# The opening of a gated linear attention and SiLU kernel in another order: pair 1's decays ahead of pair 0's logarithm

## The chip, the cores and the metric

The kernel runs on one core of a Trainium2 chip. The metric is the device time of one execution in microseconds (us); the times given are medians over several runs. TensorE (PE) does matrix products and transposes, VectorE (DVE) and ScalarE (ACT) read the accumulators in PSUM, GpSimd (POOL) works on SBUF alone, and SyncE (SP) issues most of the loads and stores. ACT and POOL issue a few as well.

## The reference

```python
def _attn_ref(q, k, v, f_logit):            # (4, 8, 768, 48) each
    f = 1.0 / (1.0 + np.exp(-f_logit))
    for t in range(S):
        state = f[:, :, t, :, None] * state + np.einsum('bhd,bhe->bhde', k[:, :, t], v[:, :, t])
        y[:, :, t] = np.einsum('bhd,bhde->bhe', q[:, :, t], state)

def _moe_ref(x, w_in, w_out):               # x (3072, 384), w_in (384, 2048), w_out (2048, 384)
    h = x @ w_in
    g = h * (1.0 / (1.0 + np.exp(-h)))
    return g @ w_out
```

x is y with the heads side by side. So each of 4 batches and 8 heads carries a 48x48 state that decays by a gate f per channel and takes up k v at each step, and the result goes through a two-layer network with SiLU.

## The kernel before

The sequence of 768 steps is cut into chunks of 128 steps (six per batch, 24 in all), and the chunks are worked on in twelve **pairs** (`PAIRS`). Pairs 0 to 3 are of kind T: the two chunks are the first two of one batch, loaded together with two neighbouring steps in one partition. The others are of kind N: the same chunk of two batches. A chunk is named by its pair and 0 or 1, so `a.1.0` is of pair 1, first chunk.

Within a chunk the recurrence becomes matrix work. The steps, with their names in the plan:

- `f`, `k`, `q`, `v`: loads (L228). `E` and `L`: exp(-f) and log(1 + that) on ACT (L234, L238), for a whole pair at once. `cs`: the running sum of the logs as a product with a triangular matrix (L305, and small products L309 that give the chunk's whole decay).
- `a`, `ia`, `al`: exponentials of that sum on ACT (L317, L256), the decays. `qg` = q times a, `ki` = k times ia (L322), written to `qk`.
- `tq`: transposes on TensorE (L329); `qkc`: the copy of them out of PSUM (L333). `sc`: the scores (L346); `at`: scores times the causal mask (L354). `vb`: v in bf16 (L184 or L182).
- `y`: the masked scores times v (L263); `yi`: the part that comes from the state before (L362). `d`: what the chunk adds to the state (L275); `sd` and `su`: the new state (L389, L387, L393).
- `yc`, `yT`, `xc`: copy, transpose and copy that give xT. `mi`: xT times w_in (L249), eight pieces of six matmuls for each pair. `si`: SiLU (L254). `mo`: times w_out (L286), `oc` and `so`: copy and store.
- `wi`, `wo`: the four requests each that bring w_in and w_out, issued by POOL (L207, L210); they turn f32 into bf16 on the way. `wi.n` feeds `mi.P.2n` and `mi.P.2n+1`.
- `idle.512.n`: n matmuls on zeros, with 512 columns each (L436).

The order of all this is the text `PLAN`, written out word by word and emitted as it stands (`manual_schedule`). A word is name, engine and buffer slot: `k.1.0:S:4` loads k of pair 1 from SP into slot 4 of k; A is ACT, V is DVE, G is POOL, P is TensorE. Each engine does its own words in the order of the plan; waits between engines, and waits for a slot whose last reader isn't done, follow from the data. An idle word names the PSUM bank that it writes. Each class of buffers has a number of slots (`SLOTS`: four for f, six for k, q and v, eight PSUM banks `pb`).

Two lines in the emission matter here. The first four loads of the plan are issued ahead of everything else, the others at their place; and the table of exp and log is loaded on ACT between the two (L457):

```python
        loads = [t for t in plan if t[0] in SRC][:4]
        for t in loads:
            run(*t)
        nc.scalar.preload_act_table_set(TABLES["exp"])
```

The load of f of pair 1 is in two halves, `f.1.0` from SP and `f.1.1` from ACT, and `E.1.0` needs both. A switch of ACT's table between exp and SiLU is put ahead of the first word that needs the other one (L485).

Of the kernel before, what the change touches and what calls it, by code (L numbers as in the profile page):

```python
# [55 lines left out]
oc.0.0:A:1 q.3.0:S:1 mo.1.0.3:P: oc.1.0:A:2 oc.1.1:V:3 qg.3.0:V:1 mi.2.6:P:4 al.5.1:A:2 qg.5.0:V:2 k.5.1:S:1 a.5.1:A:1 mi.2.0:P:1 mi.2.1:P:7
mi.2.2:P:3 q.5.1:S: qg.5.1:V:3 ia.5.1:A:2 al.5.0:A:3 a.3.1:A:4 qg.3.1:V: k.5.0:S: ia.5.0:A:0 ki.5.1:G: v.3.0:S:0 ia.3.0:A:1 ki.3.0:V: mi.2.5:P:5
tq.3.1:P:2 qkc.3.1:V:1 si.2.1:A:0 ki.5.0:G: si.2.2:A: si.2.0:A: su.2.1:G:0 mi.2.3:P:6 tq.3.0:P:0 si.2.3:A: mi.2.4:P:2 qkc.3.0:V: mi.2.7:P:1
mo.2.1.0:P:6 mo.2.1.1:P: vb.3.1:G:0 si.2.4:A: vb.3.0:V:1 d.3:P:2,0 sd.3.0:V:0 su.3.0:G:0 si.2.5:A: v.5.0:S:1 si.2.6:A: sc.3.1:P:4,5 sc.3.0:P:3,7
at.3.0.0:V:0 si.2.7:A: mo.2.1.2:P: mo.2.1.3:P: vb.5.0:G:2 at.3.1.0:V:1 mo.2.0.0:P:3 mo.2.0.1:P: mo.2.0.2:P: f.4.0:S:1 E.4.0:A:0 sd.3.1:V:0 f.6.0:S:0  # L60
qkD.5.1:S:0 at.3.1.1:V: qkD.5.0:S:1 oc.2.1:A:4 L.4.0:A:0 cs.4.1:P:5 E.6.0:A:1 L.6.0:A:1 at.3.0.1:V: v.5.1:S: sc.5.0:P:7,6 y.3:P:0,4 sc.5.1:P:2,1
at.5.0.0:V:2 yi.3.1:P: a.4.1:A:0 yc.3.0:A:0 at.5.1.1:V:0 mo.2.0.3:P: at.5.0.1:V: yc.3.1:A:1 oc.2.0:A:5 al.4.1:A:1 d.5.0:P:0 cs.6.0:P:4 a.6.0:A:1
al.6.0:A:4 yT.3.0:P:1 cs.4.0:P:7 xc.3.0:V:0 ia.6.0:A:2 yT.3.1:P:3 xc.3.1:V: q.4.0:S:1 cs.6.1:P:6 q.4.1:S: su.3.1:G:0 at.5.1.0:V: y.5.0:P:1 ia.4.1:A:4
a.6.1:A:3 mi.3.7:P:3 vb.5.1:G:0 k.4.1:S:1 ki.4.1:V:2 d.5.1:P:2 y.5.1:P:5 al.6.1:A:0 yc.5.0:A:1 yT.5.0:P:1 xc.5.0:A:1 sd.5.0:V:0 su.5.0:G:0 v.4.1:S:0
vb.4.1:G:0 mi.3.6:P:4 al.4.0:A:5 yc.5.1:V:0 yT.5.1:P:5 xc.5.1:V: ia.6.1:A:4 mi.3.3:P:1 si.3.3:A:0 q.6.0:S:0 mi.3.1:P:5 si.3.7:A: mi.5.5:P:6 si.3.6:A:
mi.3.0:P:0 mi.5.4:P:3 k.6.0:S:0 ki.6.0:G:3 mi.3.2:P:4 sd.5.1:V:1 si.5.5:A:1 mi.5.6:P:6 qg.4.1:V: si.3.0:A: mi.5.2:P:0 mi.5.7:P:1 si.5.4:A: mi.3.5:P:3
si.3.2:A: si.3.1:A: mo.3.1.0:P:5 a.4.0:A:0 mi.5.3:P:4 mo.3.1.1:P: mi.3.4:P:2 ia.4.0:A:2 si.5.2:A: v.6.0:S:2 k.4.0:S: vb.6.0:V:2 si.3.5:A: ki.6.1:G:0
mi.5.0:P:7 mi.5.1:P:3 su.5.1:G:0 mo.3.0.0:P:0 vb.6.1:V:1 si.5.6:A: d.4.1:P:6 qg.6.0:G: si.3.4:A: ki.4.0:G:1 mo.3.1.2:P: qg.4.0:V: d.6.1:P:2 v.4.0:S:
si.5.7:A: si.5.3:A: so.0.1:S: vb.4.0:A:3 si.5.1:A: d.4.0:P:4 mo.3.0.1:P: mo.3.0.2:P: sd.4.0:V:1 sd.4.1:V:0 mo.3.0.3:P: qg.6.1:G: si.5.0:A:
mo.5.0.0:P:6 mo.5.0.1:P: f.9.0:S:0 so.1.1:S: mo.3.1.3:P: f.7.0:S:1 oc.3.1:V:3 E.7.0:A:1 qkD.4.1:S:0 L.7.0:A:1 cs.7.1:P:4 mo.5.0.2:P: qkD.4.0:S:1  # L70
oc.3.0:V:0 q.7.0:S:0 sc.4.0:P:5,7 at.4.0.1:V:0 k.7.0:S:1 at.4.0.0:V: sc.4.1:P:3,1 at.4.1.0:V:2 E.9.0:A:0 al.7.1:A:2 mo.5.1.0:P:0 mo.5.1.1:P:
mo.5.1.2:P: at.4.1.1:V: y.4.0:P:3 L.9.0:A:0 ia.7.1:A:3 ki.7.1:V:1 a.7.1:A:0 cs.9.0:P:5 al.9.0:A:3 a.9.0:A:2 y.4.1:P:1 su.4.0:G:0 yc.4.1:V:0
mo.5.1.3:P: d.6.0:P:7 yc.4.0:A:1 so.2.1:S: qg.7.1:G: yT.4.0:P:1 qkD.6.0:S:2 xc.4.0:V:1 sd.6.0:V:1 su.4.1:G:0 oc.5.1:A:4 cs.7.0:P:3 al.7.0:A:5
a.7.0:A:3 cs.9.1:P:4 al.9.1:A:1 qg.7.0:G:3 ia.7.0:A:0 yT.4.1:P:0 mo.5.0.3:P: xc.4.1:V: mi.4.4:P:0 mi.4.7:P:7 a.9.1:A:1 mi.4.2:P:1 ia.9.0:A:4 so.3.0:S:
sd.6.1:V:0 oc.5.0:V:0 qkD.6.1:S:3 ia.9.1:A:3 sc.6.0:P:6,2 at.6.0.0:V:2 at.6.0.1:V: sc.6.1:P:5,3 mi.4.5:P:4 mi.4.6:P:6 si.4.5:A:1 mi.4.0:P:2 si.4.4:A:
v.7.0:S:0 vb.7.0:G:0 si.4.2:A: at.6.1.1:V:0 mi.4.1:P:3 at.6.1.0:V: y.6.1:P:1 ki.7.0:V: yc.6.1:V:0 mi.4.3:P:5 y.6.0:P:0 yc.6.0:V:1 yT.6.1:P:1 d.7.0:P:4
su.6.1:G:0 xc.6.1:V:1 su.6.0:G:0 vb.7.1:G:2 si.4.0:A: v.8.0:S:2 vb.8.1:G:1 si.4.7:A: sd.7.0:V:0 si.4.1:A: q.9.0:S:1 mo.4.1.0:P:3 si.4.3:A:
mo.4.0.0:P:0 mo.4.0.1:P: mo.4.1.1:P: mo.4.1.2:P: mo.4.0.2:P: qg.9.1:V:0 si.4.6:A: mo.4.0.3:P: f.8.0:S:0 E.8.0:A:0 L.8.0:A:0 cs.8.1:P:4 so.3.1:S:
ia.8.1:A:1 d.7.1:P:1 sd.7.1:V:1 cs.8.0:P:6 ia.8.0:A:0 mo.4.1.3:P: qkD.7.0:S:0 oc.4.0:A:3 yD.6.0:S: mi.6.2:P:1 al.8.0:A:4 qg.9.0:G:2 sc.7.0:P:0,5
# [438 lines left out]
```

## Time and profile before

| | before |
|---|---|
| time, median of 3 runs | 177.46 us (177.25 to 177.75) |
| span of the profiled execution, first to last instruction | 175.6 us |
| median of the runs less that span | 1.9 us |
| TensorE busy | 169.4 us, 96% of the span |
| ACT busy | 129.8 us, 74% |
| DVE busy | 81.2 us, 46% |
| POOL busy | 61.2 us, 35% |
| read from HBM, written | 25.17 MB, 4.72 MB |

The profile shows one execution. Its page gives the busy time of each engine; sums over stretches give the same for a part of the span, with the mean share of the 16 DMA engines; the chain of waits follows the work that ended last back from the last instruction; the order of time lists instructions by engine, merged where neighbours are alike (x6 is six in a row), with the idle time ahead of them and what ended it in brackets. Busy time of TensorE holds the idle matmuls too. A DMA's row on SPq, ACTq or POOL is its issue, not its transfer; landing times are in rows of their own. The profile gives no time of its own beside the span, so the 1.9 us are the difference to the median.

### The profile page before, as it was taken

What the parts mean: (1) busy time and instruction counts of PE and PEld (TensorE: products, weight loads), DVE (VectorE), ACT (ScalarE), POOL (GpSimd) and SP (SyncE); (2) the same over time, 40 slices, a digit from 0 to 9 for tenths busy, and PEclk for the clock granted to TensorE, in tenths of its full rate; (3) what the DMA queues carried; (4) which work ended last, traced back from release to release, by engine and by line L of the source; (5) the groups of instructions that cost most, each with busy time, mean ns of one, the idle gap of its engine ahead of it and who ended that gap; (6) DMA issues with size and microseconds to landing.
All of it is one profiled execution on the core that took longest, in us unless ns stands there. A gap on an engine that the chain in (4) does not pass through costs nothing.

```text
span 175.6 us, 4754 instructions
## 1 busy us (share of the span) xinstructions
PE 169.4 (96%) x1927; PEld 125.2 (71%) x1930; DVE 81.2 (46%) x166; ACT 129.8 (74%) x239; POOL 61.2 (35%) x104
## 2 busy tenths in 40 slices
...
GB/s 146 320 325 265 211 216 201 188 182 240 232 172 164 210 208 158 228 183 217 128 230 166 143 236 158 205 188 231 225 128 183 193 191 230 54 61 118 90 4 90
DMA packets 110677, 32.12 MB, mean 183 GB/s; under 512 B 104096, under 2 KB 110528, under 8 KB 110656
## 3 DMA queue, kind: packets, MB, share of 16 engines
...
q8 instruction: 15, 0.25, 0.6%
q14 instruction: 6, 0.05, 0.1%
HBM read 25.17 MB, written 4.72 MB: 170 GB/s over the span
## 4 chain that ended last, share of the span: by engine, by line
PE 79%; ACT 11%; DVE 5%; DMA 2%; issue 2%
PE pb L286 35%; PE pb L249 29%; ACT x L317 3%; ACT hT L254 3%; PE pb L350 3%; ACT L485 2%; DVE qk L322 2%; DMA f<-in_f_logit_dram 2%; PE pb L362 2%; PE pb L366 2%; PE pb L346 1%; PE pb L312 1%; PE pb L383 1%; PE pb L374 1%; DVE atm L354 1%
## 5 line engine op out<-in xcount | busy, mean ns | idle before, releaser
L249 PE MATMUL pb<-xT,w_in_sb 128*128 128x256 bf16 x576 | 69.1, 272 | 0.3 <-ACT hT L254 0.2
L286 PE MATMUL pb<-w_out_sb,hT 128*128 128x384 bf16 (+2 forms) x400 | 68.6, 320 | 0.0
L249 PEld LDWEIGHTS <-w_in_sb 128*128 128x128 bf16 x576 | 54.8, 98 | 9.0 <-issue 0.8
L254 ACT ACTIVATE hT<-pb 128x512 bf16<-128x512 f32 x96 | 50.5, 611 | 10.9 <-PE pb L249 10.7
L286 PEld LDWEIGHTS <-hT 128*128 128x128 bf16 x400 | 37.2, 98 | 20.5 <-issue 0.2
L393 POOL TENSOR_TENSOR st<-sd,al 48x192 bf16<-48x192 f32 x40 | 21.4, 535 | 59.0 <-PE pb L362 33.4
L354 DVE TENSOR_TENSOR atm<-pb,triu 128x512 bf16<-128x512 f32 x32 | 20.1, 684 | 11.2 <-PE pb L350 6.6
L317 ACT ACTIVATE x<-pb 128x384 f32<-128x384 f32 x48 | 21.0, 501 | 5.4 <-PE pb L305 3.0
L485 ACT ACT_TABLE_LOAD x17 | 21.8, 1283 | 0.3
L184 DVE COPY ob<-pb 128x384 f32<-128x384 f32 (+1 forms) x11 | 5.7, 528 | 27.3 <-PE pb L286 27.3
L387 DVE TENSOR_TENSOR sd<-pb,st 128x384 f32<-128x384 f32 x16 | 8.8, 552 | 11.8 <-PE pb L383 10.3
L322 POOL TENSOR_TENSOR qk<-q,x 128x384 bf16<-128x384 f32 x11 | 10.9, 996 | 9.0 <-ACT x L317 6.1
L322 POOL TENSOR_TENSOR qk<-k,x 128x384 bf16<-128x384 f32 x11 | 11.8, 1081 | 5.7 <-ACT x L317 2.4
L182 ACT COPY ob<-pb 128x384 f32<-128x384 f32 (+1 forms) x14 | 6.7, 477 | 8.5 <-PE pb L286 8.1
L234 ACT ACTIVATE e<-f 128x768 f32<-128x768 f32 x12 | 10.1, 840 | 3.8 <-DMA f<-in_f_logit_dram 3.7
L322 DVE TENSOR_TENSOR qk<-q,x 128x384 bf16<-128x384 f32 x13 | 8.2, 648 | 7.2 <-ACT x L317 7.1
L354 DVE TENSOR_TENSOR atm<-pb,mask 128x512 bf16<-128x512 f32 x16 | 10.1, 684 | 1.6 <-issue 1.0
L436 PE MATMUL pb<-zero,triu 128*128 128x512 bf16 (+1 forms) x26 | 9.0, 449 | 1.4 <-POOL triu masks.py:66 1.4
L184 DVE CAST yb<-pb 128x384 bf16<-128x384 f32 x14 | 7.6, 554 | 5.1 <-PE pb L366 2.6
L184 DVE COPY qkTT<-pb 128x1024 bf16<-128x1024 bf16 x7 | 4.6, 683 | 11.0 <-PE pb L329 11.0
L322 DVE TENSOR_TENSOR qk<-k,x 128x384 bf16<-128x384 f32 x13 | 9.0, 707 | 1.0 <-DMA k<-in_k_dram 0.8
L184 POOL CAST vb<-v 128x384 bf16<-128x384 f32 x12 | 6.4, 535 | 8.0 <-DMA v<-in_v_dram 7.7
...
## 6 DMA issues: line engine op xcount, KB each, us to landing
f<-in_f_logit_dram SPq DMA_DIRECT2D x11, 384.0 KB, 5.1
k<-in_k_dram SPq DMA_DIRECT2D x10, 384.0 KB, 5.5
q<-in_q_dram SPq DMA_DIRECT2D x10, 384.0 KB, 5.4
v<-in_v_dram SPq DMA_DIRECT2D x10, 384.0 KB, 4.9
...
w_in_sb<-in_moe_w_in_dram POOLq DMA_DIRECT2D x4, 384.0 KB, 8.6
w_out_sb<-in_moe_w_out_dram POOLq DMA_DIRECT2D x4, 384.0 KB, 10.5
...
```

The lines of the kernel that those rows point to most:

```text
L184: ENG[eng].tensor_copy(dst, src)
L234: return nc.scalar.activation(e, at("f", P)[:, j * w:(j + 1) * w], AF.Exp, scale=-1.0)
L249: nc.tensor.matmul(h[:, i, cols], w_in_sb[:, kk, n * 128:(n + 1) * 128], at("xT", P)[:, kk, cols], start=(kk == 0), stop=(kk == KT - 1))
L254: return nc.scalar.activation(at("hT", P)[:, 2 * j:2 * j + 2, :], at("h", P, j).rearrange("p (n c) -> p n c", n=2), AF.Silu)
L286: nc.tensor.matmul(at("o" + key, P, i)[:, 0:cols.stop - cols.start], at("hT", P)[:, n, i * C:(i + 1) * C], w_out_sb[:, n, cols], start=(n ...
L317: nc.scalar.activation(at(kind, P, i).rearrange("p h d -> p (h d)"), at("cs", P, i)[:, 0:HD], AF.Exp, scale=1.0 if kind == "ia" else -1.0)
L322: ENG[eng].tensor_mul(at("qk", P, i)[:, j, :, 0:D], heads("qk"[j], P, i), at("ia" if j else "a", P, i))
L354: ENG[eng].tensor_mul(at("atm", P, i)[:, r], at(f"s{r}", P, i).rearrange("p (n c) -> p n c", c=C), mask[:, None, :].to_broadcast([C, NP, C]))
L387: nc.vector.tensor_add(at("sd", P, i), d_ps, prev_state(P, i))
L393: nc.gpsimd.tensor_mul(at("st", P, i)[lo:lo + D, :, r * D:(r + 1) * D], at("sd", P, i)[lo:lo + D, :, r * D:(r + 1) * D], al_of(P, i)[lo:lo ...
L436: nc.tensor.matmul(buf["pb", int(got)][:, 0:rest[0]], triu, zero[:, 0:rest[0]], start=True, stop=True, skip_group_check=True)
L485: nc.scalar.preload_act_table_set(turns[n])
```

## The change

Only `PLAN` changes, and in it only the opening, some 235 words of 846; the 610 words from `v.3.0` on are the same in the same order, in other line breaks. The core of the diff:

```diff
-f.1.0:S:0 f.1.1:A: E.1.0:A:0 L.1.0:A:0 idle.512.10::0 cs.1.1:P:0 f.0.0:S:1 E.0.0:A:1 k.1.0:S:0 L.0.0:A:1 idle.512.1::1 cs.1.0:P:1
-q.1.0:S:0 idle.512.2::2 cs.0.0:P:2 idle.256.1::3 cs.0.1:P:3 a.1.1:A:0 qg.1.1:V:0 a.1.0:A:1 ia.1.1:A:2 ki.1.1:V: idle.512.1::4 tq.1.1:P:4 ia.1.0:A:3
-ki.1.0:V:1 v.1.0:S:0 f.2.0:S:0 qg.1.0:V: idle.512.3::5 tq.1.0:P:1 vb.1.1:V:0 vb.1.0:G:1 d.1:P:5,6 qkc.1.1:V:0 qkc.1.0:V: idle.512.1::7 idle.256.1::7
-sc.1.0:P:1,4 ia.0.0:A:0 k.0.0:S:1 ki.0.0:V:0 at.1.0.0:V:0 at.1.0.1:V: idle.512.2::7 idle.256.1::7 sc.1.1:P:7,1 at.1.1.0:V:1 at.1.1.1:V: a.0.1:A:2
-ia.0.1:A:3 sd.1.0:A:0 wi.1:G: al.1:A:0 E.2.0:A:1 L.2.0:A:1 q.0.0:S:1 a.0.0:A:1 qg.0.0:V: idle.512.1::5 cs.2.0:P:0 cs.2.1:P:5 al.2:A:1 ia.2.1:A:0
-su.1.0:G:0 ia.2.0:A:4 al.0:A:2 a.2.0:A:1 qg.0.1:V:1 idle.512.2::2 y.1:P:1,7 tq.0.0:P:4 v.0.0:S:1 yc.1.0:V:0 a.2.1:A:2 qkc.0.0:A:1 sd.1.1:V:0 wi.3:G:
-ki.0.1:G: tq.0.1:P:3 qkc.0.1:V: yT.1.0:P:1 yi.1.1:P: yc.1.1:A:0 wi.0:G: idle.512.2::2 sc.0.1:P:3,4 vb.0.1:G:0 at.0.1.0:V:0 yT.1.1:P:7 xc.1.0:A:0
-sc.0.0:P:6,5 at.0.0.1:V:1 at.0.0.0:V: vb.0.0:A:1 wi.2:G: idle.512.1::2 d.0:P:3,1 xc.1.1:A: sd.0.0:A:1 su.0.0:G:0 mi.1.2:P:7 mi.1.3:P:3 at.0.1.1:V:
-y.0:P:4,6 q.2.0:S:0 yc.0.0:A:0 yi.0.1:P: wo.0:G: mi.1.6:P:5 yT.0.0:P:4 sd.0.1:V:1 su.0.1:G:0 xc.0.0:A:1 wo.1:G: yc.0.1:V:1 yT.0.1:P:6 xc.0.1:V:
-qg.2.1:G:0 mi.1.7:P:1 k.2.0:S:0 si.1.7:A:0 mi.0.3:P:6 mi.0.7:P:4 wo.2:G: si.1.6:A: mi.0.6:P:0 mi.0.1:P:1 si.0.1:A:1 wo.3:G: su.1.1:G:0 si.0.6:A:
-mi.0.0:P:5 mi.0.2:P:2 si.0.2:A: mi.1.0:P:1 ki.2.1:V: si.1.3:A: mi.1.4:P:0 si.1.4:A: si.0.0:A: si.1.2:A: mi.0.5:P:2 mi.1.5:P:3 si.0.5:A: mi.0.4:P:0
-mi.1.1:P:7 mo.0.1.0:P:2 v.2.0:S:0 si.1.5:A: mo.0.0.0:P:3 si.1.0:A: si.1.1:A: mo.1.0.0:P:7 mo.1.1.0:P:1 mo.1.0.1:P: mo.1.1.1:P: qg.2.0:V:1 f.3.0:S:0
-si.0.3:A: mo.0.1.1:P: si.0.7:A: ki.2.0:V: tq.2.0:P:4 qkc.2.0:V:1 tq.2.1:P:6 mo.0.0.1:P: si.0.4:A: qkc.2.1:V: mo.1.1.2:P: sc.2.1:P:6,4 sc.2.0:P:0,5
-at.2.0.0:V:0 at.2.0.1:V: mo.1.0.2:P: mo.0.0.2:P: at.2.1.0:V:1 at.2.1.1:V: mo.0.1.2:P: mo.0.1.3:P: vb.2.0:G:0 vb.2.1:A:1 d.2:P:6,5 sd.2.0:V:0 E.3.0:A:1
...
+f.1.0:S:0 k.1.0:S:4 idle.512.10::4 q.1.0:S:1 f.0.0:S:1 f.1.1:A: E.1.0:A:0 L.1.0:A:0 idle.512.1::0 idle.256.1::0 cs.1.0:P:6 a.1.0:A:2 cs.1.1:P:0
+al.1:A:1 v.1.0:S:1 qg.1.0:V:0 ia.1.0:A:4 vb.1.0:G:2 ia.1.1:A:0 ki.1.0:V: ki.1.1:V:2 a.1.1:A:1 qg.1.1:V: E.0.0:A:0 idle.512.5::1 idle.256.1::1
+tq.1.0:P:6 qkc.1.0:V:1 idle.512.1::1 tq.1.1:P:5 L.0.0:A:0 idle.256.1::1 cs.0.0:P:2 ia.0.0:A:4 wi.1:G: vb.1.1:G:0 k.0.0:S:1 wi.3:G: qkc.1.1:V:
+sc.1.0:P:0,7 at.1.0.1:V:2 sc.1.1:P:4,5 at.1.1.0:V:0 cs.0.1:P:1 f.2.0:S:0 at.1.1.1:V: q.0.0:S:1 ki.0.0:G:4 a.0.0:A:2 ia.0.1:A:3 E.2.0:A:1 a.0.1:A:0
+v.0.0:S:4 d.1:P:2,7 at.1.0.0:V: idle.512.5::3 y.1:P:4,3 qg.0.0:G: qg.0.1:V:2 wi.0:G: L.2.0:A:1 tq.0.0:P:6 q.2.0:S:4 k.2.0:S:3 cs.2.0:P:5 ki.0.1:V:
+sd.1.0:A:0 tq.0.1:P:2 al.0:A:0 su.1.0:G:0 cs.2.1:P:1 yc.1.0:A:2 yT.1.0:P:0 qkc.0.0:V:0 qkc.0.1:V: ia.2.0:A:1 xc.1.0:V:3 yi.1.1:P: a.2.0:A:4 wi.2:G:
+vb.0.0:V:1 sc.0.1:P:2,4 v.2.0:S:5 a.2.1:A:0 yc.1.1:A:0 vb.0.1:G:3 al.2:A:4 idle.256.1::6 yT.1.1:P:6 ia.2.1:A:2 sc.0.0:P:5,1 d.0:P:3,0 at.0.1.1:V:1
+at.0.1.0:V: xc.1.1:A: mi.1.2:P:4 at.0.0.1:V:2 mi.1.3:P:6 at.0.0.0:V: y.0:P:5,1 yc.0.0:V:2 sd.0.0:A:0 su.0.0:G:0 yi.0.1:P: wo.0:G: wo.1:G: mi.1.6:P:2
+si.1.3:A:0 f.3.0:S:3 sd.1.1:V:1 yc.0.1:A:1 yT.0.0:P:5 yT.0.1:P:6 xc.0.1:V:1 mi.1.7:P:3 xc.0.0:A: si.1.7:A: si.1.2:A: sd.0.1:V:0 f.5.0:S:2 si.1.6:A:
+mi.0.3:P:5 mi.0.0:P:0 mi.0.2:P:7 mi.0.7:P:4 mi.0.1:P:6 mi.1.4:P:1 mi.1.5:P:3 si.1.4:A: si.0.1:A:1 ki.2.0:V:1 mi.0.5:P:2 si.0.0:A: mi.1.0:P:6 si.0.5:A:
+mi.0.4:P:0 mi.1.1:P:1 si.1.5:A: si.0.2:A: si.1.0:A: si.1.1:A: mo.0.1.0:P:2 mo.0.0.0:P:3 wo.2:G: mo.1.0.0:P:7 mi.0.6:P:6 si.0.6:A: mo.1.1.0:P:1
+si.0.3:A: si.0.7:A: ki.2.1:G:4 mo.1.0.1:P: qg.2.1:V: qg.2.0:V: mo.1.1.1:P: mo.0.1.1:P: tq.2.0:P:4 qkc.2.0:V:1 tq.2.1:P:6 mo.0.0.1:P: wo.3:G: si.0.4:A:
+qkc.2.1:V: mo.1.1.2:P: sc.2.1:P:6,4 sc.2.0:P:0,5 at.2.0.0:V:0 at.2.0.1:V: mo.1.0.2:P: mo.0.0.2:P: at.2.1.0:V:1 at.2.1.1:V: mo.0.1.2:P: mo.0.1.3:P:
+vb.2.0:G:0 vb.2.1:A:1 d.2:P:6,5 su.0.1:G:0 sd.2.0:V:0 y.2:P:4,0 mo.1.1.3:P: oc.0.1:V:0 mo.0.0.3:P: E.3.0:A:1 L.3.0:A:1 cs.3.0:P:2 yc.2.0:V:1 E.5.0:A:0
+L.5.0:A:0 a.3.0:A:4 su.2.0:G:0 sd.2.1:V:0 q.5.0:S:0 yi.2.1:P: yc.2.1:A:0 yT.2.0:P:4 cs.3.1:P:6 al.3:A:0 ia.3.1:A:1 cs.5.0:P:5 xc.2.0:V:0 a.5.0:A:0
...
```

What differs, engine by engine:

- **SP**: the first four loads are f.1.0, k.1.0, q.1.0 and f.0.0 (before: f.1.0, f.1.1, f.0.0, k.1.0). f.1.1 is no longer one of them, so ACT issues it after L457. k.0.0 goes ahead of f.2.0. Slots are other ones: q.0.0 takes slot 1, which was q.1.0's; k.1.0, v.0.0, q.2.0, k.2.0, v.2.0 and f.3.0, f.5.0 take slots that nothing has used (before, q.2.0, k.2.0, v.2.0, f.3.0 and f.5.0 took used ones).
- **ACT**: a.1.0, al.1, ia.1.0, ia.1.1 and a.1.1 stand ahead of E.0.0 and L.0.0 (before: behind). sd.1.0 moves from ahead of E.2.0 to behind L.2.0. yc.1.0 and yc.0.1 come to ACT; qkc.0.0, xc.1.0, vb.0.0 and yc.0.0 leave it. si.1.3 with its table switch stands ahead of yc.0.1 and xc.0.0.
- **DVE**: the first chunk's products come first. vb.1.1, ki.0.0, qg.0.0, yc.1.0, yc.0.1 and ki.2.1 leave it; ki.0.1, qkc.0.0, xc.1.0, vb.0.0, yc.0.0 and qg.2.1 come to it.
- **POOL**: vb.1.0, wi.1, vb.1.1, wi.3, ki.0.0, qg.0.0, wi.0, su.1.0, wi.2, vb.0.1, su.0.0, wo.0, wo.1, wo.2, ki.2.1, wo.3 (before: vb.1.0, wi.1, su.1.0, wi.3, ki.0.1, wi.0, vb.0.1, wi.2, su.0.0, wo.0, su.0.1, wo.1, qg.2.1, wo.2, wo.3).
- **TensorE**: cs.1.0 ahead of cs.1.1, tq.1.0 ahead of tq.1.1, cs.0.0 behind both, d.1 behind the scores of pair 1. The first row of ten idle matmuls stays first; one of 512 and one of 256 columns follow it, then rows of five, one and five of 512 and three more of 256 columns. In the solid part mi.0.x and mi.1.x come in another order, and mi.0.6 behind the first products with w_out.

100 lines of the change are left out of this document (49 added, 51 removed).

## The prediction

> **What bounds the kernel now.** I read the page's shares first, then sums over stretches of the span, then the chain of waits, and then the order of time engine by engine in the part that the change touches, and last the landing times of single DMA requests. All times are microseconds from the start of the span. The first row is the page's; the next two are sums over two stretches, from 1 to 22 and from 22 to 172; the fourth is the same first stretch for line 436 alone, the idle matmuls.
>
> ```profile
> PE 169.4 (96%) x1927; PEld 125.2 (71%) x1930; DVE 81.2 (46%) x166; ACT 129.8 (74%) x239; POOL 61.2 (35%) x104
> ```
>
> ```profile
> 1.00:22.00 21.00, 19.23 (x285) 11.44 (x289) 15.82 (x48) 15.05 (x30) 10.32 (x26) 1.00 1.11 265
> 22.00:172.00 150.00, 149.65 (x1640) 113.50 (x1638) 64.99 (x118) 114.38 (x208) 50.46 (x74) 1.00 0.88 174
> ```
>
> ```profile
> 1.00:22.00 21.00, 9.03 (x26) 2.85 (x29) 1.00 1.11 265
> ```
>
> The columns are length, busy PE, weight loads, DVE, ACT, POOL, the granted clock, the share of the DMA engines and GB/s. From 22 on TensorE is busy 149.65 of 150, so nothing there can be won by reordering, and what is won ahead of it is kept if its operands come in time. Before 22 it is busy 19.23 of 21, but 9.03 of that are idle matmuls. So the opening is bound by something else, and the chain of waits names it: the loads of f, then ACT, then DVE. The rows of TensorE:
>
> ```profile
> 19.41 1.48 PE L249 MATMUL pb<-xT,w_in_sb 128*128 128x256 bf16 x12
> 20.83 0.57 PE L263 MATMUL pb<-vb,atm 64*128 64x48 bf16 x32
> ...
> 22.51 8.68 PE L249 MATMUL pb<-xT,w_in_sb 128*128 128x256 bf16 x78
> ```
>
> The first row is mi.1.2 and mi.1.3 (pair 1's x times w_in), the second y.0, the third the solid stretch from mi.1.7 on. **The measure of the change is by how much that 22.51 moves.** Now ACT and DVE ahead of it:
>
> ```profile
> 0.74 0.47 ACTq L228 DMA_DIRECT2D f<-in_f_logit_dram  x1
> 1.25 1.28 ACT L457 ACT_TABLE_LOAD   x1 [1.25 <-PEq L502]
> 4.20 0.84 ACT L234 ACTIVATE e<-f 128x768 f32<-128x768 f32 x1 [1.67 <-DMA f<-in_f_logit_dram]
> 5.08 0.84 ACT L238 ACTIVATE lf<-e 128x768 bf16<-128x768 f32 x1
> 5.82 0.83 ACT L234 ACTIVATE e<-f 128x768 f32<-128x768 f32 x1
> 6.68 0.84 ACT L238 ACTIVATE lf<-e 128x768 bf16<-128x768 f32 x1
> 7.43 2.41 ACT L317 ACTIVATE x<-pb 128x384 f32<-128x384 f32 x6
> ```
>
> ```profile
> 7.94 0.56 DVE L322 TENSOR_TENSOR qk<-q,x 128x384 bf16<-128x384 f32 x1 [3.73 <-ACT x L317]
> ...
> 10.69 1.28 DVE L184 COPY qkTT<-pb 128x1024 bf16<-128x1024 bf16 x2
> 11.89 0.55 DVE L322 TENSOR_TENSOR qk<-k,x 128x384 bf16<-128x384 f32 x1
> 12.48 2.48 DVE L354 TENSOR_TENSOR atm<-pb,mask 128x512 bf16<-128x512 f32 x4
> ```
>
> ```profile
> 5.97 0.48 PE L305 MATMUL pb<-lf,tincl 128*128 128x384 bf16 x2 [0.53 <-ACT lf L238]
> ```
>
> ACT waits for f until 4.20, then does exp and log of pair 1 and, before any decay, exp and log of pair 0 (5.82 to 7.52). DVE's first product waits 3.73 for that. At 11.89 a product of pair 0 (ki.0.0) stands between pair 1's transposes and its masked products.
>
> **The change, part by part.**
>
> *Decays of pair 1 first.* The log of pair 1 ends at 5.92; TensorE's prefix sum takes 0.48 (the 5.97 row), so a.1.0 can start at 6.5 where the first decay started at 7.43: 0.9 earlier. E.0.0 and L.0.0 (0.84 each) go behind pair 1's five small activations, at about 8.3 to 10.0; their decays are wanted by POOL at 11.7, which hides them.
>
> *ki.0.0 off DVE.* 0.55 leaves the place between the copies and the masked products; about 0.5 of it counts, since the scores must come in between anyhow. Together 1.4: DVE's four masked products (2.48) run from 11.05 to 13.55 instead of 12.48 to 14.96.
>
> *From there to the solid stretch.* Before, 19.41 - 14.96 = 4.45 pass from the last masked product to mi.1.2, and 22.51 - 19.41 = 3.10 from there to mi.1.7. The new order has the same kinds of work in both, but ACT now has sd.1.0, yc.1.0 and the decays of pair 2 behind L.2.0 before yc.1.1, and sc.0.0 takes the bank that ia.2.1 must have read; laying these out at the durations above I get 4.6 instead of 4.45, and 3.1 again. That gives mi.1.2 at 18.15 and mi.1.7 at 21.25: 1.25 earlier.
>
> *Queues.* SP's and POOL's rows of the stretch that is reordered, and landing times of single requests (KB and us to landing, one row for each): first v.0.0 (issued at 8.97) with the first w_in request (9.56), then q.2.0 (10.53), k.2.0 (11.49) and k.1.0 (1.79).
>
> ```profile
> 1.79 0.58 SPq L228 DMA_DIRECT2D k<-in_k_dram  x1
> ...
> 7.77 1.15 SPq L228 DMA_DIRECT2D q<-in_q_dram  x1
> 8.97 1.11 SPq L228 DMA_DIRECT2D v<-in_v_dram  x1
> 10.53 0.93 SPq L228 DMA_DIRECT2D q<-in_q_dram  x1
> ```
>
> ```profile
> 9.08 0.54 POOL L184 CAST vb<-v 128x384 bf16<-128x384 f32 x1 [5.17 <-DMA v<-in_v_dram]
> 9.56 0.91 POOL L207 DMA_DIRECT2D w_in_sb<-in_moe_w_in_dram  x1
> 12.30 1.08 POOL L393 TENSOR_TENSOR st<-sd,al 48x192 bf16<-48x192 f32 x2 [1.83 <-ACT al L256]
> 13.33 0.81 POOL L207 DMA_DIRECT2D w_in_sb<-in_moe_w_in_dram  x1
> 14.21 0.99 POOL L322 TENSOR_TENSOR qk<-k,x 128x384 bf16<-128x384 f32 x1
> ```
>
> ```profile
> v<-in_v_dram SPq DMA_DIRECT2D x1, 384.0 KB, 4.9
> w_in_sb<-in_moe_w_in_dram POOLq DMA_DIRECT2D x1, 384.0 KB, 6.5
> ```
>
> ```profile
> q<-in_q_dram SPq DMA_DIRECT2D x1, 384.0 KB, 7.8
> ```
>
> ```profile
> k<-in_k_dram SPq DMA_DIRECT2D x1, 384.0 KB, 11.0
> ```
>
> ```profile
> k<-in_k_dram SPq DMA_DIRECT2D x1, 384.0 KB, 4.8
> ```
>
> k.1.0 and q.1.0 each move one request up and f.0.0 goes to the fourth place; v.1.0 still is the sixth 384 KB, so vb.1.0 and the first w_in request stay at 9.08 and 9.56. The second follows vb.1.1 at about 10.9 instead of 13.33. Then come ki.0.0 and qg.0.0 on POOL, 0.99 each, from 11.7 to 13.7 and so just within DVE's masked products; the third w_in request waits behind them and still leaves at 13.7, earlier than before. su.1.0 (1.08) ends near 15.8, after which yi.1.1 and yc.1.1 are free in time.
>
> q.0.0 now takes q.1.0's slot, so SP waits for pair 1's last q product (about 9.15) and issues it at 9.2 instead of 7.77, with v.0.0, q.2.0, k.2.0, v.2.0 and pair 3's f queued behind. The ring is still full then, so q.0.0 itself lands where it did, near 12.7 (7.77 + 4.9). v.0.0 goes out at 10.2 and so behind the first w_in request, as q.2.0 did. Bounds for it: 4.9 (v.0.0's own row) and 11.0 (k.2.0's), that is 15.1 and 21.2. Nearest is q.2.0, which had v.0.0 (13.9) and w_in (16.0) ahead of it and landed at 18.3, steps of 2.2 and 2.3; with q.0.0 at 12.7 ahead instead, v.0.0 lands at 12.7 + 4.5 = 17.2. vb.0.0 stands on DVE at 16.5, ahead of pair 0's masked products: 0.65 late, of which mi.1.2 and mi.1.3 (1.48) on TensorE cover about 0.3. Cost 0.35.
>
> [...]
>
> *f.1.1.* It is no longer among the first four loads, so ACT issues it behind the table load. Both are started by ACT's queue, and nothing the load writes is read by the issue, so I take 0.8 for the issue and 4.2 for the landing, cost 0; the other end is the table's end at 2.0 and worse (first rival).
>
> *At nothing:* si.1.3 with its table load (1.28) ahead of yc.0.1 on ACT lies under mi.1.3 and y.0; the fourth w_out request waits on POOL for ki.2.1 and so for k.2.0, by its row 11.0 after about 12.4, and w_out is first read after the solid stretch of w_in (22.51 + 8.68). Idle matmuls only fill.
>
> Sum: 0.9 + 0.5 - 0.15 - 0.35 = 0.9 less. The profiled execution has a span of 175.6, 1.9 under the median of 177.46; its sum goes over to the median: 176.6.
>
> **The rivals.** *f.1.1 waits for the table load (slower).* For it: POOL's w_in issue at 9.56 starts only as the cast before it ends (9.62). Against it: POOL's issue is the one engine whose issues count as work. Then f.1.1 leaves at 2.0 behind k.1.0 and q.1.0, and lands when 1152 KB have, as k.1.0 did: 1.79 + 4.8 = 6.6, so 2.4 later on the chain: 1.25 - 2.4 = 1.15 lost, 178.6 (v.0.0 then is early enough). It decides from a landing at 5.4 on.
>
> [...]
>
> *v.0.0 is squeezed by the two w_in requests (no change).* For it: k.2.0's 11.0. Against it: only one w_in request leaves before v.0.0. From a landing at 18.0 the gain is gone, 177.4; at the far end, 21.2, it would be 180.7, which I give little.
>
> *The gain is given back later.* The DMA engines' share is 0.88 after 22 with TensorE full; loads that are bound by them can't move up by 0.9 with the rest. Against it: TensorE waits 0.35 in 150, so most loads have slack. Time 177.2.
>
> **How the numbers follow.** A difference under 0.3% (0.53) can't be told from no change. Chances: forecast 0.55 (its own range 175.9 to 176.9), still better 0.05, v.0.0 squeezed 0.15, given back 0.10, f.1.1 behind the table 0.13, k.2.0's far end 0.02. So faster 0.60, same 0.25, slower 0.15. The range from 175.9 to 178.0 leaves out the slower cases and little else.
>
> **What would show it.** Right: f.1.1 issued near 0.8 and landed near 4.2; first decay at 6.5, masked products from 11.0, mi.1.2 at 18.1, y.0 near 19.8, solid stretch from 21.6; v.0.0 landed by 17.2. Wrong: exp of pair 1 after 5; DVE idle ahead of vb.0.0 until 18 or later with TensorE idle before y.0; POOL's qg.0.0 waiting for q.0.0 beyond 13.1; or an early solid stretch and yet the same end, with new waits for DMA after 40.

## The result, and the profile after

| | before | after |
|---|---|---|
| median time | 177.61 us (177.25 to 177.85) | 176.45 us (175.95 to 178.73) |
| ratio of after to before, 95% interval | | 0.9933 (0.9906 to 0.996) |
| span of the profiled execution | 175.6 us | 174.2 us |
| first decay on ACT | 7.43 | 6.52 |
| pair 1's masked products on DVE | 12.48 | 11.04 |
| mi.1.2, y.0, solid stretch (mi.1.7) | 19.41, 20.83, 22.51 | 18.19, 19.60, 21.35 |

The change gains 1.16 us, 0.7% (by the interval 0.7 to 1.7 us), and the solid stretch starts 1.16 earlier. The two agree, though to the last digit only by chance: the spans of the two profiled executions differ by 1.4. Executions far above the others of their kernel (one of four here, 178.73; six of fourteen in the third experiment) count in the medians but not in the ratios. The line numbers of the changed kernel are one smaller than before.

The same sums over stretches as before, now to 170.6. TensorE is still full after 22 (148.40 of 148.60), so what the opening gained was kept:

```profile
1.00:22.00 21.00, 19.35 (x298) 12.39 (x298) 15.83 (x49) 15.97 (x31) 13.18 (x29) 1.00 1.11 254
22.00:170.60 148.60, 148.40 (x1626) 112.45 (x1625) 65.28 (x117) 112.04 (x205) 49.84 (x73) 1.00 0.88 178
```

The order of time on ACT and on DVE, the opening. f.1.1 leaves ACT's queue at 0.77 while the table load runs, and the first decay follows the first prefix sum instead of pair 0's logarithm:

```profile
0.74 1.28 ACT L456 ACT_TABLE_LOAD   x1 [0.74 <-PEq L501]
0.77 0.48 ACTq L227 DMA_DIRECT2D f<-in_f_logit_dram  x1
4.23 0.84 ACT L233 ACTIVATE e<-f 128x768 f32<-128x768 f32 x1 [2.21 <-DMA f<-in_f_logit_dram]
5.10 0.84 ACT L237 ACTIVATE lf<-e 128x768 bf16<-128x768 f32 x1
6.52 0.49 ACT L316 ACTIVATE x<-pb 128x384 f32<-128x384 f32 x1 [0.57 <-PE pb L304]
```

```profile
7.04 0.56 DVE L321 TENSOR_TENSOR qk<-q,x 128x384 bf16<-128x384 f32 x1 [2.84 <-ACT x L316]
7.61 1.03 DVE L321 TENSOR_TENSOR qk<-k,x 128x384 bf16<-128x384 f32 x2
8.56 0.55 DVE L321 TENSOR_TENSOR qk<-q,x 128x384 bf16<-128x384 f32 x1
9.03 1.49 DVE L183 COPY qkTT<-pb 128x1024 bf16<-128x1024 bf16 x2
11.04 2.48 DVE L353 TENSOR_TENSOR atm<-pb,mask 128x512 bf16<-128x512 f32 x4 [0.52 <-PE pb L345]
```

TensorE, from mi.1.2 to the solid stretch:

```profile
18.19 1.48 PE L248 MATMUL pb<-xT,w_in_sb 128*128 128x256 bf16 x12
19.60 0.58 PE L262 MATMUL pb<-vb,atm 64*128 64x48 bf16 x32
...
21.35 2.82 PE L248 MATMUL pb<-xT,w_in_sb 128*128 128x256 bf16 x24
```

SP's queue and POOL's rows where they meet: q.0.0 and v.0.0 (the first two rows), and then the two w_in requests with the casts of v ahead of each. q.0.0 leaves 0.38 before the first w_in request.

```profile
9.14 0.37 SPq L227 DMA_DIRECT2D q<-in_q_dram  x1
9.56 0.57 SPq L227 DMA_DIRECT2D v<-in_v_dram  x1
```

```profile
9.07 0.50 POOL L183 CAST vb<-v 128x384 bf16<-128x384 f32 x1 [5.16 <-DMA v<-in_v_dram]
9.52 0.91 POOL L206 DMA_DIRECT2D w_in_sb<-in_moe_w_in_dram  x1
10.43 0.52 POOL L183 CAST vb<-v 128x384 bf16<-128x384 f32 x1
10.87 0.79 POOL L206 DMA_DIRECT2D w_in_sb<-in_moe_w_in_dram  x1
```

Their landings (KB, us after the issue): q.0.0 3.5 and so 12.67; v.0.0 5.8, 15.35.

```profile
q<-in_q_dram SPq DMA_DIRECT2D x1, 384.0 KB, 3.5
```

```profile
v<-in_v_dram SPq DMA_DIRECT2D x1, 384.0 KB, 5.8
```

### The profile page after: what moved, and what is told of

Read it like the earlier page. It is cut to its first block, busy times and chain, and to the rows that moved or that the text cites. A ratio compares the mean times of both kernels' runs of the same rounds, so it can differ in the third digit from the quotient of the medians.

```text
span 174.2 us, 4746 instructions
## 1 busy us (share of the span) xinstructions
PE 168.2 (97%) x1927; PEld 125.2 (72%) x1927; DVE 81.5 (47%) x166; ACT 128.6 (74%) x237; POOL 63.4 (36%) x106
## 4 chain that ended last, share of the span: by engine, by line
PE 85%; ACT 7%; DVE 2%; DMA 2%; issue 1%; ACTq 0%
PE pb L285 35%; PE pb L248 32%; ACT hT L253 3%; PE pb L349 3%; ACT L484 2%; PE pb L361 2%; PE pb L328 2%; DMA f<-in_f_logit_dram 2%; PE pb L365 2%; PE pb L373 2%; PE pb L311 2%; PE pb L345 1%; ACT x L316 1%; PE pb L382 1%; PE pb L262 1%; DVE atm L353 1%
## 5 line engine op out<-in xcount | busy, mean ns | idle before, releaser
L392 POOL TENSOR_TENSOR st<-sd,al 48x192 bf16<-48x192 f32 x40 | 21.9, 549 | 48.4 <-PE pb L361 34.1
L321 POOL TENSOR_TENSOR qk<-k,x 128x384 bf16<-128x384 f32 x12 | 13.0, 1094 | 12.8 <-DMA k<-in_k_dram 9.7
L321 DVE TENSOR_TENSOR qk<-q,x 128x384 bf16<-128x384 f32 x13 | 9.0, 710 | 5.8 <-ACT x L316 5.7
L321 DVE TENSOR_TENSOR qk<-k,x 128x384 bf16<-128x384 f32 x12 | 8.0, 677 | 6.7 <-DMA k<-in_k_dram 6.6
L183 DVE CAST yb<-pb 128x384 bf16<-128x384 f32 x13 | 7.1, 555 | 6.7 <-ACT hT L253 3.1
L183 POOL CAST vb<-v 128x384 bf16<-128x384 f32 x13 | 7.0, 542 | 8.4 <-DMA v<-in_v_dram 8.0
L435 PE MATMUL pb<-zero,triu 128*128 128x512 bf16 (+1 forms) x26 | 7.5, 424 | 1.4 <-POOL triu masks.py:66 1.4
L181 ACT CAST yb<-pb 128x384 bf16<-128x384 f32 x11 | 5.3, 488 | 4.3 <-PE pb L365 4.3
```

Source lines behind the costliest of these rows:

```text
L181: nc.scalar.copy(dst, src)
L183: ENG[eng].tensor_copy(dst, src)
L321: ENG[eng].tensor_mul(at("qk", P, i)[:, j, :, 0:D], heads("qk"[j], P, i), at("ia" if j else "a", P, i))
L392: nc.gpsimd.tensor_mul(at("st", P, i)[lo:lo + D, :, r * D:(r + 1) * D], at("sd", P, i)[lo:lo + D, :, r * D:(r + 1) * D], al_of(P, i)[lo:lo ...
```

## The experiments

Ratios are to the kernel before, run beside each on the same chip; 0.9933 is the changed kernel. 0.001 is 0.18 us. "Masked" is the start of pair 1's masked products, "solid" that of the solid stretch, in the one profiled execution; they are left out where that execution was one far above the others.

| | ratio (95%) | median | masked | solid |
|---|---|---|---|---|
| 1 f.0.0 ahead of k, q | 1.030 (1.0267 to 1.0333) | 182.97 | | |
| 2 and pair 0's exp, log first | 1.0269 (1.0229 to 1.0309) | 182.06 | 12.19 | 27.99 |
| 3 ki.0.0 on DVE | 0.9987 (0.9966 to 1.0008) | 177.61 | | |
| 4 second w_in request later | 1.003 (1.0013 to 1.0047) | 177.86 | 11.12 | 22.71 |
| 5 q.0.0 in its own slot | 0.9955 (0.9931 to 0.9978) | 176.54 | 11.46 | 21.78 |
| 6 = 1 with own slot | 0.9987 (0.9978 to 0.9995) | 177.10 | 12.11 | 22.43 |
| 7 = 2 with own slot | 0.9995 (0.9985 to 1.0005) | 177.23 | 12.18 | 22.50 |
| 8 = 3 with own slot | 0.9972 (0.995 to 0.9993) | 176.84 | 12.27 | 22.58 |
| 9 exp and log in halves, own slot | 0.9967 (0.9946 to 0.9989) | 177.14 | | |
| 10 no idle matmuls, own slot | 1.0154 (1.0125 to 1.0183) | 179.79 | 12.62 | 23.23 |
| 11 f.1.1 late, own slot | 1.0058 (1.0037 to 1.0079) | 178.50 | 13.94 | 24.25 |
| 12 = 9, w_in behind the cast | 0.9955 (0.9932 to 0.9979) | 176.51 | 10.50 | 20.98 |

### 1 and 2: the orders of the loads and of ACT undone

```diff
-f.1.0:S:0 k.1.0:S:4 idle.512.10::4 q.1.0:S:1 f.0.0:S:1 f.1.1:A: E.1.0:A:0 L.1.0:A:0 ... a.1.1:A:1 qg.1.1:V: E.0.0:A:0 ... L.0.0:A:0
+f.1.0:S:0 f.0.0:S:1 k.1.0:S:4 idle.512.10::4 q.1.0:S:1 f.1.1:A: E.1.0:A:0 L.1.0:A:0 ... a.1.1:A:1 qg.1.1:V: E.0.0:A:0 ... L.0.0:A:0
```

The second one also has `E.0.0:A:1 L.0.0:A:1` right behind `L.1.0` (and `E.2.0:A:0`, `L.2.0:A:0`, so that the slots alternate).

> The changed kernel with one load put back: pair 0's f ahead of pair 1's k and q. Theory A (the chain f, ACT, DVE up to pair 1's masked products sets the solid stretch, and the new order of ACT needs q.1.0 early): q.1.0 lands near 7.8 instead of 6.62, the first decay stays at 6.5, but DVE's first product starts at 7.9 instead of 7.04, masked products at 11.75, solid stretch at 22.0 to 22.1, 0.7 more: about 177.15. The prediction's own pricing (the order of loads at nothing, the decays 0.9 by themselves): no change, 176.45. Theory B (the gain is the second w_in request, which landed at 19.7 instead of 21.3): no change.

> As before this one (pair 0's f ahead of k and q) and pair 0's exp and log ahead of pair 1's decays again; the rest of the change stays. Theory A: first decay at 7.4, first product at 7.95, masked products at 11.8, solid stretch at 22.1, 0.8 more: about 177.25. That is, with the old loads the order of ACT is worth only 0.1. If the decays were worth 0.9 by themselves, as the prediction summed it: 0.9 more than with the loads alone undone. Theory B: no change, 176.45.

They lost 6.5 and 6.0 us against the changed kernel (0.0367 and 0.0336), eight or nine times what theory A had. The second one's rows show where: q.0.0 is issued at 10.29, behind the first w_in request (9.80), and takes 6.7 to land instead of 3.5. TensorE then waits 3.32 for pair 0's product of it, and after that wait its granted clock (the first number behind the five engines) is 0.50 for six microseconds:

```profile
10.29 0.37 SPq L227 DMA_DIRECT2D q<-in_q_dram  x1
```

```profile
q<-in_q_dram SPq DMA_DIRECT2D x1, 384.0 KB, 6.7
```

```profile
18.63 1.04 PE L328 MATMUL pb<-ident,qk 128*128 128x128 bf16 x8 [3.32 <-POOL qk L321]
```

```profile
15.00:18.00 3.00, 0.31 (x26) 0.20 (x16) 0.84 (x2) 1.16 (x4) 0.83 (x1) 0.93 1.18 233
18.00:24.00 6.00, 5.37 (x63) 4.17 (x67) 3.65 (x7) 2.40 (x7) 3.60 (x6) 0.50 1.20 270
```

q.0.0 waits on SP because it reuses q.1.0's slot: it leaves when pair 1's last q product ends. So 1.15 of lateness on DVE became 4.4 in its landing. What happens in the queues is seen in the packets of the changed kernel, first from 10.5 to 12 and then, w_in's packets having come, from 15 to 16.5 (packets, MB, share of the 16 engines; q1 holds SP's loads, q0 POOL's):

```profile
q1 hardware_dynamic: 1279, 0.48, 116.5%
```

```profile
q0 software_dynamic: 229, 0.22, 87.0%
q1 hardware_dynamic: 211, 0.08, 30.9%
```

The two queues got nearly the same number of packets (229 and 211). POOL's packets are larger (0.22 MB in 229 of them, against 0.08 MB in 211) and take most of the engines' time (87.0% against 30.9%), and SP's loads fall from 0.48 MB to 0.08 MB in 1.5 us, a sixth. The loads of SP that weren't complete when w_in's packets began, at 13.1, took far longer: q.2.0, k.2.0 and v.2.0, issued at 10.18, 11.52 and 12.71, landed after 12.8, 17.5 and 21.3, where q.0.0 took 3.5.

### 3: ki.0.0 on DVE

```diff
-qkc.1.1:V: sc.1.0:P:0,7 ... ki.0.0:G:4
+qkc.1.1:V: ki.0.0:V:4 sc.1.0:P:0,7
```

> The changed kernel with pair 0's first k product on DVE again, between pair 1's transposes and its masked products. Theory A: it waits for its decay (to 11.0), takes 0.55, and the masked products start at 11.55 instead of 11.04; solid stretch at 21.85, 0.5 more: 176.95. Theory B: no change (w_in leaves at the same time or earlier, since POOL has one product less).

The ratio is 0.0054 over the changed kernel, 1.0 us where 0.5 was expected. But it holds only eight of the fourteen runs (176.54 to 177.92); the other six took 179.26 to 184.05. The profiled execution is one of the six (182.75), and it shows what befell the second experiment: q.0.0 is issued at 10.25, behind the first w_in request (9.76), lands at 17.1, and TensorE waits for pair 0's product of it.

```profile
10.25 0.37 SPq L227 DMA_DIRECT2D q<-in_q_dram  x1
```

```profile
18.73 1.04 PE L328 MATMUL pb<-ident,qk 128*128 128x128 bf16 x8 [3.24 <-POOL qk L321]
```

Nothing of the edit stands ahead of that moment; up to pair 1's last q product, which frees the slot, the order is that of the changed kernel. What is later in this execution is TensorE's rate: the two matmuls of the first prefix sum take 0.53 each instead of 0.32 (the tenth experiment comes back to that), DVE's first product starts at 7.66 instead of 7.04, and the last q product, which takes 0.86 instead of 0.55 beside a cast on POOL, ends at 10.23 instead of 9.11. So the changed kernel, which stands 0.38 us ahead of the request, can be expected to miss it too at times. Its one run of 178.73 and the fourth experiment's one of 181.31 may be such cases, but no profile shows them, and why the third has so many is open. With q.0.0 in a slot of its own (fifth to eighth) two of 42 runs are above 178 (178.26 and 181.53).

### 4: the two w_in requests apart

```diff
-wi.1:G: vb.1.1:G:0 k.0.0:S:1 wi.3:G: ... qg.0.0:G: wi.0:G:
+wi.1:G: vb.1.1:G:0 k.0.0:S:1 ... qg.0.0:G: wi.3:G: wi.0:G:
```

> The changed kernel with the second w_in request behind POOL's two products of pair 0, issued near 13.0 (before: 13.33) instead of 10.87; everything else keeps its order. Theory A alone: masked products at 11.04 as now, the request lands near 21.0 to 21.4, and if w_in has slack the time stays at 176.45. Theory B: mi.1.6, the first reader, waits for it and starts at 21.0 to 21.4 instead of 20.29, the solid stretch at 22.0 to 22.3, 0.7 to 1.0 more: 177.2 to 177.4. Both can hold, that is the gain needs the chain and the request.

0.0097, 1.7 us, over the changed kernel (1.4 in the medians, and 1.36 at the solid stretch), more than expected. TensorE's rows: mi.1.6 waits 0.65 for w_in, as theory B said, and ahead of it yi.1.1 waits 0.40 for POOL, since su.1.0 now stands behind two requests in a row (13.88 to 15.46):

```profile
16.65 0.33 PE L361 MATMUL pb<-st,qkTT 128*128 128x96 bf16 x4 [0.40 <-POOL st L392]
...
21.71 0.83 PE L248 MATMUL pb<-xT,w_in_sb 128*128 128x256 bf16 x6 [0.65 <-DMA w_in_sb<-in_moe_w_in_dram]
```

So not all of the loss is w_in's: mi.1.2, ahead of its wait, starts at 18.80 instead of 18.19, and the run doesn't price the two causes apart. The profile of before does it for w_in: there the second request landed 8.0 after its issue at 13.33, that is at 21.3, and mi.1.6, which reads it, starts at 20.29 in the changed kernel. With that landing it would have to wait for about 1.0. The earlier second request is needed for the gain; it is not its source, for the masked products were early in this run too (11.12) and nothing came of it.

### 5 to 8: the same edits with q.0.0 in a slot of its own

```diff
-q.0.0:S:1
+q.0.0:S:2
```

> The changed kernel with one number changed: pair 0's q is loaded into a slot of its own and no longer waits on SP for pair 1's last q product. Theory C (that wait stands just ahead of a step: issued up to 0.4 us before the first w_in request q.0.0 lands at 12.7, issued after it at 17): q.0.0 leaves near 7.8 and lands at 12.7, v.0.0 at 13.9, nothing on the path moves, ratio to the kernel before 0.993 as the change has it. Rival D (v.0.0 and q.0.0 ahead of w_in cost w_in its place): w_in's first two requests land 1 later than 17.1 and 19.7, mi.1.6 waits, ratio 0.997.

> The first experiment (pair 0's f ahead of pair 1's k and q) with pair 0's q in a slot of its own. Theory C (most of the 6 us that it lost were the late issue of q.0.0): q.0.0 lands at 12.7 again, first product at 7.9, masked products at 11.75, 0.7 over the changed kernel: ratio to the kernel before 0.997. Rival E (the late q.1.0 itself costs what was lost): ratio 1.03 as it was.

> The second experiment (f of pair 0 ahead of k and q, and its exp and log ahead of pair 1's decays) with pair 0's q in a slot of its own. Theory C with A: 0.1 more than the kernel with the loads alone undone and 0.8 more than the changed one: ratio 0.998. If the decays are worth 0.9 whatever the loads are: ratio 1.002. Rival E: 1.027 as it was.

> The third experiment (pair 0's first k product on DVE again) with pair 0's q in a slot of its own. Theory A: masked products 0.5 later, solid stretch at 21.85, ratio to the kernel before 0.996, in every run (the third experiment's runs were spread over 7 us). Rival E: the same spread.

Theory C holds. With that one number changed, the loss of the first edit falls from 1.030 to 0.9987 and that of the second from 1.0269 to 0.9995; q.0.0 left at 7.8 to 7.9 and landed at 12.7 or 12.8 in all four profiles. For the changed kernel itself the slot makes no difference that can be told (0.9955, within its interval of 0.9933).

Now the parts can be priced against the fifth, 176.54. The order of the loads undone: 0.56 (expected 0.7). The order of ACT undone as well: 0.13 more, not 0.9, which the overlapping intervals can't tell from nothing, and the time is that of the kernel before. So the two orders together are worth 0.69 of the 0.80 that the fifth gains over its own runs of before (177.34). The fourth case, the new loads with the old order of ACT, was not run. DVE's rows of the sixth and the seventh show why: with the old loads the first product waits for q.1.0 in the one and for its decay in the other, and both begin at 7.9 to 8.0:

```profile
7.92 0.56 DVE L321 TENSOR_TENSOR qk<-q,x 128x384 bf16<-128x384 f32 x1 [3.71 <-DMA q<-in_q_dram]
```

```profile
7.98 0.56 DVE L321 TENSOR_TENSOR qk<-q,x 128x384 bf16<-128x384 f32 x1 [3.77 <-ACT x L316]
```

ki.0.0 on DVE costs 0.30 in the medians, where 0.5 was expected; the intervals (0.9972 and 0.9955) overlap, so the size is not shown. The solid stretch of the one profiled execution is 0.80 later than in the fifth, of which 0.19 is there already at the first product (7.66 and 7.47).

### 10: no idle matmuls

Every `idle` word is taken out.

> The changed kernel with pair 0's q in a slot of its own and without any idle matmul. The prediction's step (idle matmuls only fill): no change, ratio 0.9955. Theory G (they raise TensorE's rate before the first prefix sum: a 128x512 matmul of the row takes 0.43 at first and 0.21 later, and the moment of the step lies between 4.0 and 7.2 in the profiles so far): the prefix sums, transposes and scores run at the slow rate until some 4 us after the first real matmul, that is to 10 or later; first decay at 7.1 instead of 6.5, masked products 1 later, ratio 1.000 to 1.003, and more if the rate falls again in the gaps.

0.0199, 3.5 us, over the fifth (3.25 in the medians): the step "idle matmuls only fill" is wrong. TensorE's first real work runs at the slow rate, a row of eight transposes in 1.11 instead of 0.61, and scores, second transposes and masked products follow late (12.62):

```profile
6.00 0.48 PE L304 MATMUL pb<-lf,tincl 128*128 128x384 bf16 x1 [6.00 <-ACT lf L237]
...
8.36 1.11 PE L328 MATMUL pb<-ident,qk 128*128 128x128 bf16 x8 [0.74 <-ACT x L316]
```

That accounts for 1.2 to 1.5 in the profiled execution, 177.93, which was the quickest of them; what the others lost beyond it no profile shows.

The first row of TensorE in the changed kernel and in the fifth experiment shows the same thing from another side. The same twelve matmuls, which start 0.43 apart at the slow rate and 0.22 apart at the fast one, took 3.96 in the one and 5.09 in the other:

```profile
1.37 3.96 PE L435 MATMUL pb<-zero,triu 128*128 128x512 bf16 x12 [1.37 <-POOL triu masks.py:66]
6.00 0.32 PE L304 MATMUL pb<-lf,tincl 128*128 128x384 bf16 x1 [0.67 <-ACT lf L237]
```

```profile
1.37 5.09 PE L435 MATMUL pb<-zero,triu 128*128 128x512 bf16 x12 [1.37 <-POOL triu masks.py:66]
6.25 0.50 PE L304 MATMUL pb<-lf,tincl 128*128 128x384 bf16 x1
```

In the fifth experiment the row itself is in the way of the prefix sum, whose first matmul then still runs at the slow rate (0.50 for 0.32): first product at 7.47 instead of 7.04, solid stretch at 21.78 instead of 21.35. The step from the slow rate to the fast one fell at 4.0 in the changed kernel's execution and behind 6.89 in the eighth's, where the prefix sum's matmul at 6.57 still takes 0.53 and the two at 6.89 take 0.63 instead of 0.49. What sets its moment is not shown. With the old order this makes no difference: the seventh's row took 5.09 too, and its decays began at 7.44, as they did before (7.43), since they stand behind pair 0's logarithm.

### 11: f.1.1 late

```diff
-f.1.1:A:   (behind f.0.0)
+f.1.1:S:   (behind k.1.0, among the first four loads)
```

> The changed kernel with pair 0's q in a slot of its own and the second half of pair 1's f issued by SP behind pair 1's k, so that it lands late as the prediction's first rival had it. By the rival's price (each us of f.1.1 is a us of the chain, the gain is gone from a landing at 5.4 on): f.1.1 lands near 5.3, exp starts at 5.35 instead of 4.23, first decay at 7.65, masked products at 12.1, ratio to the kernel before 1.000 to 1.002. If the chain has slack there: less than 0.5 lost, ratio under 0.998.

f.1.1 landed at 5.93, not 5.3, and exp started at 6.02, 1.70 later than in the fifth (4.32). The time is 1.83 us higher (0.0103): the chain has no slack there.

```profile
6.02 0.84 ACT L233 ACTIVATE e<-f 128x768 f32<-128x768 f32 x1 [4.00 <-DMA f<-in_f_logit_dram]
```

That this looks like one for one is partly luck. In the profiled execution the first decay is 1.43 later than in the fifth (8.38 and 6.95), but the masked products and the solid stretch are 2.48 and 2.47 later. In between TensorE, whose first row of idle matmuls had run out, had waited 2.16 for the logarithm, and its granted clock was then 0.50 for some three microseconds (the first number behind the five engines):

```profile
7.79 0.32 PE L304 MATMUL pb<-lf,tincl 128*128 128x384 bf16 x1 [2.16 <-ACT lf L237]
```

```profile
8.10:11.40 3.30, 3.30 (x19) 1.48 (x17) 2.15 (x4) 2.64 (x7) 1.48 (x2) 0.50 1.11 302
```

So the run mixes the lateness of f.1.1 with a slower TensorE; the price of the lateness alone is not shown.

### 9 and 12: a shorter chain

```diff
-E.1.0:A:0 L.1.0:A:0 idle.512.1::0 idle.256.1::0 cs.1.0:P:6 a.1.0:A:2 ... ia.1.0:A:4 ... ki.1.0:V:
+E.1.0:A:0 E.1.1:A: L.1.0:A:0 L.1.1:A: cs.1.0:P:6 ia.1.0:A:4 ki.1.0:V:0 a.1.0:A:2 ...
```

The twelfth also has `vb.1.1:G:0 wi.1:G:` for `wi.1:G: vb.1.1:G:0`.

> The changed kernel with pair 0's q in a slot of its own, pair 1's exp and log in two halves each (the first exp starts when the first half of f has landed), pair 1's first k decay and product ahead of its first q, and the two idle words between the first row and the prefix sums gone. Theory A (the chain f, ACT, DVE still sets the solid stretch): log ends at 5.45 instead of 5.95, last product near 8.5 to 8.9, masked products 0.4 to 0.6 earlier, solid stretch 0.3 earlier; ratio to the kernel before 0.992 to 0.993. Theory F (pair 0's q, landed at 12.7, and w_in are next in line): masked products earlier, but the solid stretch where it was, ratio 0.9955 as with the own slot alone.

> The kernel with the split exp and log, own slot and short first row, and one word moved: the first w_in request behind POOL's second cast of pair 1's v, so that it is issued near 10.1 instead of 9.6 and its first packets come near 13.6 instead of 13.1. Theory H (a load on SP's queue that is not complete when w_in's packets start is served at a fraction of its rate; with the split kernel v.0.0 was caught by that at times, landing at 18.25, and TensorE waited for its cast): v.0.0 lands by 14.0, no wait for vb.0.0, solid stretch near 21.0 to 21.2, the runs closer together, median 176.0 to 176.3, ratio to the kernel before 0.993 to 0.994. Theory F alone (pair 0's q and the two w_in landings bind): first w_in request lands 0.5 later, mi.1.2 waits for it, ratio 0.996 to 0.998 as the split kernel had.

Neither is better than the changed kernel; intervals overlap all round. The ninth's profiled execution is one far above its median, so it shows only what can happen: v.0.0 issued at 9.06, landed 9.2 later, TensorE waiting 0.64 for its cast. The twelfth removed that (v.0.0 landed after 4.9) and has the earliest solid stretch of all, 20.98, but a median of 176.51 where 176.0 to 176.3 was expected. Two waits that the changed kernel doesn't have come later:

```profile
20.98 3.26 PE L248 MATMUL pb<-xT,w_in_sb 128*128 128x256 bf16 x28
...
100.54 0.40 PE L349 MATMUL pb<-qkT 48*128 48x128 bf16 x8 [0.43 <-DMA qkT<-qk]
106.19 0.81 PE L285 MATMUL pb<-w_out_sb,hT 128*128 128x384 bf16 x4 [0.47 <-DVE yb L183]
```

and SP's loads ahead of them left when they had left in the changed kernel, though the work was 0.37 ahead (the twelfth, then the changed kernel):

```profile
30.25 4.80 SPq L227 DMA_DIRECT2D q<-in_q_dram  x1
...
43.32 1.45 SPq L227 DMA_DIRECT2D v<-in_v_dram  x2
```

```profile
30.26 4.80 SPq L227 DMA_DIRECT2D q<-in_q_dram  x1
...
43.33 1.46 SPq L227 DMA_DIRECT2D v<-in_v_dram  x2
```

So the loads stand still when the opening is shortened further. But the second of these rows stood at 43.56 before the change as well, and the 1.16 of the change were kept all the same. That the two late waits come from the loads, and not from that one execution (177.05, above its median), is not shown: no run took it apart.

## Why the prediction was right, step by step

**Decays first, 0.9.** First decay forecast at 6.5, seen at 6.52; DVE's first product went from 7.94 to 7.04. The size is right, but two conditions were priced at nothing. The order of the loads, "k.1.0 and q.1.0 each move one request up", is what lets DVE use the early decay: without it the new order of ACT is worth 0.13 (sixth against seventh), no more than noise. Nor could the loads alone have done it: before, the first product waited for its decay (the 7.94 row), not for q. And the 6.5 took the prefix sum at 0.48, TensorE's fast rate; in executions where the fast rate begins later, it is 7.0 to 7.1 (6.95 in the fifth, 7.13 in the sixth).

**ki.0.0 off DVE, 0.5.** The total of the two terms, 1.44 from 12.48 to 11.04, came as forecast (1.4), but not from where it said; that the second term has the right size is luck. From the end of the second copy to the first masked product it was 0.51 before, with ki.0.0 in between (11.97 to 12.48), and 0.52 after without it (10.52 to 11.04): the scores had to come in between either way. Before, the scores of the first chunk ended at 12.44, and so did ki.0.0, which therefore had cost nothing:

```profile
12.02 0.42 PE L346 MATMUL pb<-qkTT 48*64 48x128 bf16 x16
```

The 0.54 came from two rows of before that the prediction didn't use:

```profile
8.70 1.33 DVE L322 TENSOR_TENSOR qk<-k,x 128x384 bf16<-128x384 f32 x2 [0.20 <-ACT x L317]
...
10.42 0.35 DVE L184 CAST vb<-v 128x384 bf16<-128x384 f32 x1
```

The cast vb.1.1 went to POOL: 0.27, from its start to that of the copies. The k products wait no more for their decays, about 0.20, and take 1.03 instead of 1.33, 0.30: before, the second one took 0.86 while POOL cast the other half of v (9.08 to 9.62). Against that the way from the first copy to the masked products grew by 0.22 (1.79 before, 2.01 now). The eighth experiment's 0.30 is not the price of ki.0.0 as it stood, since its decay comes later now.

**4.6 and 3.1 to the solid stretch.** Seen: 18.19 - 13.52 = 4.67, and 3.16.

**v.0.0, 0.35.** This is the term that was mis-sized. It was to land at 17.2, and landed at 15.35; vb.0.0 ran on DVE at 16.48 without a wait, and the cost was 0. The step took the ring as full, that is an issue on SP at 1.1 as before (1.15 and 1.11 in the rows at 7.77 and 8.97); the issues of q.0.0 and v.0.0 took 0.37 and 0.57, and v.0.0 left at 9.56, with the first w_in request and not behind it. These 0.35, less 0.13 by which the two paths above came out longer than forecast, and 0.04 more ahead of them, make the difference between the forecast 0.9 and the 1.16 seen. The 4.9 behind the lower bound of 15.1 was no case of a load that shared its time with w_in: in the profile of before that request's first packets came at 13.2, 3.6 after its issue, and v.0.0 landed at 13.86.

**q.0.0 at 9.2, landing near 12.7.** In the profiled execution seen 9.14 and 12.67. The number was right, but the full ring that it was put down to doesn't show in the issue, which took only 0.37 where it had taken 1.15 before: the load ahead of it, f.2.0, landed at 11.48, and q.0.0 came 1.2 behind that. And the step held by 0.4 us only: once behind w_in, q.0.0 lands at 17.0, and that cost 4.9 us (second experiment against seventh); the third fell over the edge in an execution whose order up to there is the changed kernel's. The second rival looked for this cliff at v.0.0 and left out that q.0.0, which DVE and POOL need sooner, stands nearer to it.

**f.1.1 during the table load, cost 0.** Seen: issue at 0.77, landing at 4.14. The rival didn't come about; that its price is about right is borne out by the eleventh, though not apart from the granted clock, 0.50 for some three microseconds there.

**At nothing.** si.1.3 and its table load (18.86 to 20.14) lay under mi.1.3 and y.0 as said; the fourth w_out request waited for k.2.0 until 30.45 and landed at 38.23, where it had landed at 38.22. "Idle matmuls only fill" was wrong (tenth). The earlier second w_in request had no price at all in the sum, and most of the gain hangs on it (fourth).

**Given back later.** Not here: 1.16 at the solid stretch and 1.16 in the median. With a still earlier opening it may begin (twelfth).
